# A DMA from SBUF to SBUF in place of PE transposes for the stacked q of a gated linear attention with an MLP

## The chip, the cores and the metric

The kernel runs on one core of a Trainium2 chip. The metric is the device time of one execution in microseconds; the time of a kernel is the median of several executions. A profile is one more execution, with its own time; its page counts from the first to the last instruction, and this stretch is called the span.

## The reference

Batch B = 4, heads H = 8, sequence S = 768, head size D = 48; the MLP works on DM = H * D = 384 and 4 * DM = 1536 columns.

```python
mag = np.sqrt(a_re * a_re + a_im * a_im)
scale = np.minimum(mag, 0.999) / (mag + 1e-06)
a_re_n, a_im_n = (a_re * scale, a_im * scale)
for t in range(S):
    ar, ai = (a_re_n[:, :, t, :, None], a_im_n[:, :, t, :, None])
    new_re = ar * S_re - ai * S_im
    new_im = ar * S_im + ai * S_re
    kv = np.einsum('bhd,bhe->bhde', k[:, :, t], v[:, :, t])
    S_re, S_im = (new_re + kv, new_im)
    y[:, :, t] = np.einsum('bhd,bhde->bhe', q[:, :, t], S_re)
x = y.transpose(0, 2, 1, 3).reshape(B, S, H * D)
mu = np.mean(x, axis=-1, keepdims=True)
var = np.mean((x - mu) ** 2, axis=-1, keepdims=True)
xn = (x - mu) / np.sqrt(var + 1e-06) * g_ln
out = x + np.maximum(xn @ w_ch1, 0.0) @ w_ch2
```

The recurrence has a complex decay per channel; only the real part of the state is read. The inputs and the output are float32.

## The kernel before

The sequence of each batch is cut into chunks of 128 rows (6 a batch, 24 in all, numbered 0 to 23). Three chunks are a unit (UC = 3; 8 units, two a batch, numbered 0 to 7). The recurrence is worked as attention within a chunk and a state from chunk to chunk.

For a unit, `elementwise` computes on ACT and DVE the decay's cumulated magnitude (`ep`, `en`, lines 179 to 185) and phase (`n`, `f`, lines 197 to 208), its cosine and sine, and then writes two stacked tiles in bfloat16: `qstk`, which holds for each of the 128 rows, 3 chunks and 8 heads the 48 values of q times cosine and, after a gap of 16, the 48 of q times sine (128 columns a head, with zeros in the gaps), and `kstk`, the same for k. Lines 233 to 238 write qstk first, then kstk. There are two of each, for even and odd units.

For each chunk:
- `heads_t` (line 245) brings both to a layout with the 128 stacked columns on the partitions. For q, PE transposes the 8 heads into PSUM (`q_ps`, line 250), and ACT copies them to `qt` in SBUF (line 252). For k, PE does 8 more (`k_ps`, line 255), and DVE copies them to `kt` (line 257). `qt` and `kt` have two buffers each.
- `scores` (line 260) multiplies kt with qt for each head (`a_ps`, line 267), and DVE masks the result into `at` (line 269).
- `values` (line 272) adds at times v and qt times the state `s` (`y_ps`, lines 278 and 281), which ACT copies to `x` (line 284), and then makes the next state (`t_ps`, lines 297 to 304). Line 281 is the last that reads a chunk's qt.
- `norm_t` (line 310) takes the mean and variance of x (`stats`, `mv`, `mean`, lines 317 to 320) and transposes x into `xt` (lines 322 to 327).

The MLP runs a unit or two behind: `up` (line 338; `h_ps`, line 344, and its Relu on ACT into `ht`, line 346) for the unit before, and `down` (line 348; `o_ps`, line 352, `o`, line 355, and the DMA to the output, line 358) for the one before that.

The main loop (lines 407 to 435) walks over the chunks in slots; `heads_t` of the next chunk comes between `scores` and `values` of this one, and `advance` and `need` feed in pieces of `elementwise` of later units. A scheduler orders the instructions of each engine when the program is built and adds the waits; on the chip each engine works its list in that order.

SP's DMA queue carries the loads of `a_re` and `a_im` (tiles `ar` and `ai`, lines 100 and 103; each batch's next but one is loaded while the kernel runs), the small copies `edge` (line 189) and the outputs (line 358). POOL's queue loads q, k, v (to bfloat16) and the weights.

Of the kernel before, what the change touches and what calls it, by code (L numbers as in the profile page):

```python
# [10 lines left out]
BF16 = mybir.dt.bfloat16  # L11
# [3 lines left out]
PI = 3.14159265358979323846  # L15
LNCAP = -0.0020010006671670786
MAGIC = 12582912.0
TWO_PI_SAFE = 6.2831845
INV2PI = 1.0 / (2.0 * PI)
NOSYNC = mybir.DependencyInfo(mybir.DependencyClass.NoSync, mybir.DependencyReason.DATA)  # L20
# [3 lines left out]
def kernel(  # L24
# [12 lines left out]
    nc = tc.nc  # L37
    B, H, S, D = q.shape
    C = 128
# [6 lines left out]
    UC = 3  # L46
# [5 lines left out]
    psum = pool("psum", 1, space=bass.MemoryType.PSUM)  # L52
# [9 lines left out]
    ident = consts.tile([C, C], BF16)  # L62
# [48 lines left out]
    for i in range(2):  # L111
        qs = consts.tile([C, UC, H, 2, DP], BF16, name=f"qstk{i}")
        ks = consts.tile([C, UC, H, 2, DP], BF16, name=f"kstk{i}")
# [19 lines left out]
    def table(inst):  # L133
        tc.add_manual_dep(inst.ins, group[0].ins.name, NOSYNC, reason="table order")
        group[1].append(inst.ins)
        return inst
# [15 lines left out]
    def elementwise(b, us, carry):  # L152
# [44 lines left out]
        for st in us:  # L197
            n, f, af = (utile(x, tag="tmp", bufs=4) for x in ("n", "f", "af"))
            for c in range(UC):
# [3 lines left out]
                if carry[0] is not None:  # L203
                    nc.tensor.matmul(ps, lhsT=all_turn, rhs=carry[0], start=False, stop=True)
                nc.vector.tensor_scalar(out=row(n, c), in0=ps, scalar1=MAGIC, scalar2=MAGIC,  # L205
                                        op0=ALU.add, op1=ALU.subtract)
                st["fdone"] = nc.vector.tensor_tensor(out=row(f, c), in0=ps, in1=row(n, c),  # L207
                                                      op=ALU.subtract)
                if st["u"] * UC + c < NCH - 1:
                    if carry[0] is None:  # L210
                        carry[0] = row(st["th"], c)
                    else:
# [7 lines left out]
            sin, cos = utile("sin"), utile("cos")  # L220
            table(nc.scalar.activation(out=sin, in_=f, func=AF.Sin, scale=TWO_PI_SAFE))  # L221
            table(nc.scalar.activation(out=cos, in_=af, func=AF.Sin, scale=-TWO_PI_SAFE,
                                       bias=half_pi))
# [21 lines left out]
    def heads_t(g):  # L245
        st, c = units[g // UC], g % UC
        qs, ks = st["qs"], st["ks"]
        q_ps = psum.tile([C, H, C], BF16, tag="tr", name="q_ps", bufs=2)
        for h in range(H):
            nc.tensor.transpose(q_ps[:, h], qs[:, c, h].rearrange("p a d -> p (a d)"), ident)  # L250
        qt = att.tile([C, H, C], BF16, tag="qt", name="qt")
        nc.scalar.copy(out=qt, in_=q_ps)  # L252
        k_ps = psum.tile([C, H, C], BF16, tag="tr", name="k_ps", bufs=2)
        for h in range(H):
            nc.tensor.transpose(k_ps[:, h], ks[:, c, h].rearrange("p a d -> p (a d)"), ident)  # L255
        kt = att.tile([C, H, C], BF16, tag="kt", name="kt")
        nc.vector.tensor_copy(out=kt, in_=k_ps)  # L257
        chunks[g] = dict(qt=qt, kt=kt)

    def scores(g):  # L260
# [143 lines left out]
    load_weights()  # L404
    load(1, ("q", "k", "v"))
    heads_t(0)
    for s in range(NG + 2 * UC):
        U, c = s // UC, s % UC
        up_u, dn_u = U - 1, U - 2
        hasup, hasdn = 0 <= up_u < NUT, 0 <= dn_u < NUT  # L410
        js = [c * (NJ // UC) + i for i in range(NJ // UC)]
        if s < NG:
            scores(s)
        advance(RATE)
        if hasup:
            up(up_u, js[0])
            up(up_u, js[1])
        if s + 1 < NG:
            need((s + 1) // UC)
            heads_t(s + 1)  # L420
        if s < NG:
            values(s)
            done[0] = (s + 1) // UC
            if s % NCH == NCH - 1:
                load(s // NCH + 2, ("v",))
        advance(RATE)
        if hasup:
            up(up_u, js[2])
            up(up_u, js[3])
        if hasdn:  # L430
            down(dn_u, c)
        if s < NG:
            norm_t(s)
            if s % NCH == HOLD:
                hold_a(s // NCH + 2, mark[0])
# [30 lines left out]
```

## Time and profile before

| | |
|---|---|
| time before, median of 3 | 266.68 us (265.99 to 268.78) |
| profiled execution, its own time | 267.18 us |
| its span | 265.4 us |
| PE busy | 195.5 us (74%) |
| weight loads (PEld) | 128.0 us (48%) |
| DVE busy | 193.1 us (73%) |
| ACT busy | 161.0 us (61%) |
| POOL busy | 49.5 us (19%) |
| transposes of q on PE (L250) | 19.1 us, 192 matmuls |
| evictions of q on ACT (L252) | 24.3 us, 24 copies of 1011 ns |
| DMA, POOL's queue | 76112 packets, 9.44 MB, 62.3% of 16 engines |
| DMA, SP's queue | 25536 packets, 14.18 MB, 23.7% of 16 engines |

A line of the group table gives the source line (L250), the engine, the operation with the tile written and the tiles read, the shapes, the count, then the busy time in us and the mean duration of one in ns, and last the idle time of the engine just before, with what ended most of it. PEld is the load of the stationary operand, which can run beside a matmul. In a line of the timeline the first number is the start in us, the second the duration. In a line of stages, the columns after the length of the stage are each engine's busy us, with the number of instructions, then the TensorE clock that was granted (1.00 is full speed), the busy share of the DMA engines and the GB/s moved. The chain of waits goes back from the last instruction through whatever released each step.

### The profile page before, as it was taken

What the parts mean: (1) busy time and instruction counts of PE and PEld (TensorE: products, weight loads), DVE (VectorE), ACT (ScalarE), POOL (GpSimd) and SP (SyncE); (2) the same over time, 40 slices, a digit from 0 to 9 for tenths busy, and PEclk for the clock granted to TensorE, in tenths of its full rate; (3) what the DMA queues carried; (4) which work ended last, traced back from release to release, by engine and by line L of the source; (5) the groups of instructions that cost most, each with busy time, mean ns of one, the idle gap of its engine ahead of it and who ended that gap; (6) DMA issues with size and microseconds to landing.
All of it is one profiled execution on the core that took longest, in us unless ns stands there. A gap on an engine that the chain in (4) does not pass through costs nothing.

```text
span 265.4 us, 4671 instructions
## 1 busy us (share of the span) xinstructions
PE 195.5 (74%) x1860; PEld 128.0 (48%) x1860; DVE 193.1 (73%) x395; ACT 161.0 (61%) x250; POOL 49.5 (19%) x61
## 2 busy tenths in 40 slices
PE   0012467429782395999998788999977999998994
PEld 0000355217460273666664455666644676764452
DVE  2145896787975989987899979958998876652111
ACT  3244945469995449886973599869636454543320
POOL 9844900035304006001003200010002001001000
PEclk9999999658997579799999689999997999999999
DMA  8999999999989908920379900000100000000012
GB/s 129 149 135 135 181 227 231 204 122 119 131 121 210 140 1 43 159 39 32 91 178 193 77 0 33 30 34 2 61 5 25 32 32 30 33 30 32 30 59 90
DMA packets 102070, 23.91 MB, mean 90 GB/s; under 512 B 87840, under 2 KB 101664, under 8 KB 102048
## 3 DMA queue, kind: packets, MB, share of 16 engines
q0 software_dynamic: 76112, 9.44, 62.3%
q1 hardware_dynamic: 25536, 14.18, 23.7%
q8 instruction: 14, 0.23, 0.3%
q10 hardware_dynamic: 400, 0.00, 0.1%
q14 instruction: 8, 0.07, 0.1%
HBM read 28.31 MB, written 4.72 MB: 124 GB/s over the span
## 4 chain that ended last, share of the span: by engine, by line
PE 38%; ACT 28%; DVE 23%; issue 5%; DMA 3%; SPq 1%; POOLq 0%; POOL 0%; DVEq 0%; ACTq 0%
PE o_ps L352 12%; PE h_ps L344 9%; ACT L128 4%; ACT ht L346 4%; DVE n L205 4%; ACT qt L252 3%; DVE f L207 3%; DMA ai<-in_a_im_dram 3%; ACT ep L184 3%; PE a_ps L267 3%; PE q_ps L250 3%; ACT ai L168 2%; ACT th L195 2%; ACT en L185 2%; PE k_ps L255 2%
## 5 line engine op out<-in xcount | busy, mean ns | idle before, releaser
L344 PE MATMUL h_ps<-xt,w1b 128*128 128x384 bf16 x288 | 63.0, 338 | 5.4 <-ACT ht L346 3.0
L346 ACT ACTIVATE ht<-h_ps 128x384 bf16<-128x384 f32 x96 | 45.8, 496 | 31.6 <-PE h_ps L344 30.7
L352 PE MATMUL o_ps<-w2b,ht 128*128 128x384 bf16 x288 | 51.3, 326 | 1.4 <-ACT ht L346 1.2
L352 PEld LDWEIGHTS <-ht 128*128 128x128 bf16 x288 | 27.8, 97 | 19.4 <-issue 1.9
L344 PEld LDWEIGHTS <-w1b 128*128 128x128 bf16 x288 | 26.1, 100 | 21.9 <-issue 9.6
L355 DVE SCALAR_TENSOR_TENSOR o<-o_ps,rs,x 128x384 f32<-128x384 f32 x24 | 14.8, 615 | 25.4 <-PE o_ps L352 18.1
L269 DVE TENSOR_TENSOR at<-a_ps,mask 128x512 bf16<-128x512 f32 x48 | 31.6, 675 | 1.0 <-PE a_ps L267 1.0
L252 ACT COPY qt<-q_ps 128x1024 bf16<-128x1024 bf16 x24 | 24.3, 1011 | 13.0 <-PE q_ps L250 12.9
L250 PE MATMUL q_ps<-ident,qstk 128*128 128x128 bf16 x192 | 19.1, 251 | 12.5 <-DVE qstk L236 11.6
L257 DVE COPY kt<-k_ps 128x1024 bf16<-128x1024 bf16 x24 | 16.5, 688 | 10.6 <-PE k_ps L255 10.5
L332 POOL TENSOR_SCALAR rs<-mv 128x3 f32<-128x3 f32 x8 | 1.9, 233 | 113.1 <-DVE o L355 80.5
L250 PEld LDWEIGHTS <-qstk 128*128 128x128 bf16 x192 | 15.1, 114 | 16.2 <-DVE qstk L236 14.2
L201 PE MATMUL th_ps<-th,u_turn 128*128 128x384 bf16 x24 | 9.3, 395 | 17.0 <-DVE f L207 8.6
L183 PE MATMUL l_ps<-lm,u_half 128*128 128x384 bf16 x24 | 8.3, 361 | 18.3 <-DVE lm L176 17.4
L278 PE MATMUL y_ps<-v,at 128*128 128x48 bf16 x192 | 16.0, 189 | 6.1 <-DVE at L269 4.9
L221 ACT ACTIVATE sin<-f 128x1152 bf16<-128x1152 bf16 x8 | 9.3, 1163 | 15.7 <-DVE f L207 11.9
L284 ACT CAST x<-y_ps 128x384 bf16<-128x384 f32 x24 | 11.6, 484 | 11.3 <-PE y_ps L278 11.2
L278 PEld LDWEIGHTS <-at 128*128 128x128 bf16 x192 | 12.6, 99 | 11.7 <-DVE at L269 9.3
L255 PE MATMUL k_ps<-ident,kstk 128*128 128x128 bf16 x192 | 17.6, 245 | 0.8 <-DVE kstk L236 0.6
L267 PE MATMUL a_ps<-qt,kt 128*128 128x128 bf16 x192 | 17.2, 234 | 0.7 <-DVE kt L257 0.4
L184 ACT ACTIVATE ep<-l_ps 128x384 bf16<-128x384 f32 x24 | 12.2, 508 | 9.1 <-PE l_ps L183 9.0
L165 DVE TENSOR_TENSOR r<-ai,rec 128x1152 bf16<-128x1152 f32 x8 | 10.8, 1350 | 9.3 <-DMA ai<-in_a_im_dram 9.3
(77 smaller groups left out, 383.4 us busy)
## 6 DMA issues: line engine op xcount, KB each, us to landing
out_dram<-o SPq DMA_DIRECT2D x24, 192.0 KB, 1.9
q<-in_q_dram POOLq DMA_DIRECT2D x3, 576.0 KB, 10.5
k<-in_k_dram POOLq DMA_DIRECT2D x3, 576.0 KB, 11.1
v<-in_v_dram POOLq DMA_DIRECT2D x3, 576.0 KB, 9.1
ar<-in_a_re_dram SPq DMA_DIRECT2D x6, 192.0 KB, 3.5
ai<-in_a_im_dram SPq DMA_DIRECT2D x6, 192.0 KB, 8.3
w1b<-in_moe_w_ch_dram POOLq DMA_DIRECT2D x1, 1152.0 KB, 13.6
w2b<-in_moe_w_ch_dram POOLq DMA_DIRECT2D x1, 1152.0 KB, 22.0
```

The costliest lines, as they stand in the source:

```text
L184: table(nc.scalar.activation(out=row(ep, c), in_=ps, func=AF.Exp))
L250: nc.tensor.transpose(q_ps[:, h], qs[:, c, h].rearrange("p a d -> p (a d)"), ident)
L252: nc.scalar.copy(out=qt, in_=q_ps)
L255: nc.tensor.transpose(k_ps[:, h], ks[:, c, h].rearrange("p a d -> p (a d)"), ident)
L257: nc.vector.tensor_copy(out=kt, in_=k_ps)
L267: nc.tensor.matmul(a_ps[:, j], lhsT=ch["kt"][:, h], rhs=ch["qt"][:, h], start=True, stop=True)
L269: nc.vector.tensor_tensor(out=at[:, ts(i, H // 2)], in0=a_ps, in1=mask_b, op=ALU.mult)
L278: nc.tensor.matmul(y_ps[:, h], lhsT=ch["at"][:, h], rhs=vt[:, h, gb], start=True, stop=sp is None)
L344: nc.tensor.matmul(h_ps, lhsT=w1b[:, i, ts(j, C)], rhs=st["xt"][:, i], start=(i == 0), stop=(i == ND - 1))
L346: nc.scalar.activation(out=st["ht"][:, j], in_=h_ps, func=AF.Relu)
L352: nc.tensor.matmul(o_ps, lhsT=st["ht"][:, j, ts(c, C)], rhs=w2b[:, j], start=(j == 0), stop=(j == NJ - 1))
L355: nc.vector.scalar_tensor_tensor(out=o, in0=o_ps, scalar=st["rs"][:, ds(c, 1)], in1=chunks[U * UC + c]["x"], op0=ALU.mult, op1=ALU.add)
```

## The change

From unit 1 on (chunks 3 to 23), the stacked q of a chunk, 128 rows by 8 heads of 128 columns, is transposed by one DMA on SP's queue from `qstk` straight into `qt`. The 8 PE transposes, their PSUM tile and the copy by ACT are gone for these chunks. The first three chunks, and k in all chunks, stay as they were. In the changed file the DMA has line 253.

```diff
+XBAR = (0,)
...
     def heads_t(g):
         st, c = units[g // UC], g % UC
         qs, ks = st["qs"], st["ks"]
-        q_ps = psum.tile([C, H, C], BF16, tag="tr", name="q_ps", bufs=2)
-        for h in range(H):
-            nc.tensor.transpose(q_ps[:, h], qs[:, c, h].rearrange("p a d -> p (a d)"), ident)
         qt = att.tile([C, H, C], BF16, tag="qt", name="qt")
-        nc.scalar.copy(out=qt, in_=q_ps)
-        k_ps = psum.tile([C, H, C], BF16, tag="tr", name="k_ps", bufs=2)
-        for h in range(H):
-            nc.tensor.transpose(k_ps[:, h], ks[:, c, h].rearrange("p a d -> p (a d)"), ident)
         kt = att.tile([C, H, C], BF16, tag="kt", name="kt")
-        nc.vector.tensor_copy(out=kt, in_=k_ps)
+        for i, (o, x) in enumerate(((qt, qs), (kt, ks))):
+            if g >= UC and i in XBAR:
+                nc.sync.dma_start_transpose(out=o, in_=x[:, c].rearrange("p h a d -> p (h a d)"))
+                continue
+            t_ps = psum.tile([C, H, C], BF16, tag="tr", name="qk_ps", bufs=2)
+            for h in range(H):
+                nc.tensor.transpose(t_ps[:, h], x[:, c, h].rearrange("p a d -> p (a d)"), ident)
+            if i == 0:
+                nc.scalar.copy(out=o, in_=t_ps)
+            else:
+                nc.vector.tensor_copy(out=o, in_=t_ps)
         chunks[g] = dict(qt=qt, kt=kt)
```

## The prediction

> **What bounds the kernel now.** I read the page first (busy shares, slices, groups), then the chain of waits by stage, then the busy time of stages, and last the timeline around the start of a unit, because there the stacked q is finished just before it is used.
>
> ```profile
> PE 195.5 (74%) x1860; PEld 128.0 (48%) x1860; DVE 193.1 (73%) x395; ACT 161.0 (61%) x250; POOL 49.5 (19%) x61
> ...
> L252 ACT COPY qt<-q_ps 128x1024 bf16<-128x1024 bf16 x24 | 24.3, 1011 | 13.0 <-PE q_ps L250 12.9
> L250 PE MATMUL q_ps<-ident,qstk 128*128 128x128 bf16 x192 | 19.1, 251 | 12.5 <-DVE qstk L236 11.6
> ```
>
> No engine bounds the whole span: PE and DVE are both near 73%. The removed work is in the two last lines: 19.1 us of PE and 24.3 us of ACT for 24 chunks. The busy time of four stages (the columns are us of the stage, then PE, PEld, DVE, ACT, POOL) tells where that work counts:
>
> ```profile
> 61.00:91.00 30.00, 18.50 (x187) 11.32 (x187) 24.53 (x49) 23.89 (x39) 8.03 (x6) 0.84 1.82 153
> 94.00:141.00 47.00, 43.17 (x438) 29.13 (x437) 42.41 (x85) 37.99 (x61) 6.29 (x5) 0.94 0.72 84
> 150.00:180.00 30.00, 27.76 (x284) 18.46 (x282) 25.29 (x49) 25.60 (x43) 1.11 (x2) 0.93 0.06 21
> 210.00:236.00 26.00, 25.91 (x307) 18.22 (x306) 16.62 (x38) 12.88 (x24) 1.11 (x2) 1.00 0.09 32
> ```
>
> From 210 on PE alone is full. From 94 to 180 PE and DVE are both near 90%. From 61 to 91 DVE and ACT are at 80% and wait for each other. Next, the timeline at the start of unit 4 (start, us, engine, line):
>
> ```profile
> 140.70 0.75 DVE L236 TENSOR_TENSOR qstk<-qe,sin 128x1152 bf16<-128x1152 bf16 x1
> ...
> 142.04 0.75 DVE L236 TENSOR_TENSOR kstk<-ke,sin 128x1152 bf16<-128x1152 bf16 x1
> ...
> 143.91 0.68 DVE L257 COPY kt<-k_ps 128x1024 bf16<-128x1024 bf16 x1
> ...
> 144.64 0.45 PEld L267 LDWEIGHTS <-kt 128*128 128x128 bf16 x8 [0.50 <-DVE kt L257]
> ```
>
> qstk is complete at 141.45, but the scores (L267) start only at 144.64, when kt is there. So a new way for q has a cover of 3.1 us: the k path takes that long anyway. Units 1, 2 and 6 look the same (qstk 58.40, 90.84, 193.91; kt done 61.56, 94.00, 197.04). Units 3, 5 and 7 have their qstk 12 us or more early (unit 3 at 102.5 against L250 at 117.2).
>
> **The change, part by part.** *Removed:* for 21 of 24 chunks 8 transposes (19.1/24 = 0.80 us of PE) and one eviction (1.01 us of ACT), in all 16.7 us of PE and 21.2 us of ACT. What of it sets the end, by stage:
> - 210 to 236: the L250 rows in this stage are 2.60 us of PE, and PE is full: 2.6 us.
> - 150 to 180: the chain of this stage gives 13.1% to qt and 3.7% to q_ps, 5.0 us together. The k transposes and kt follow a step later and take part of it over; the PE time removed is 2.55. Between the two: 3.8 us.
> - 94 to 141: 3.2% and 2.8% of 47 us, 2.8 us. DVE is 90% busy and is not relieved: half, 1.4 us.
> - 61 to 91: one qt of 0.90 us lies on the chain: half, 0.5 us.
>
> The sum is 8.3 us, at most 11.3 if nothing takes the place of the removed pieces.
>
> *Added:* 21 transposing DMAs of 256 KB on SP's queue. The trace has no such transfer, so its time T from issue to landing has to be bounded:
>
> ```profile
> out_dram<-o SPq DMA_DIRECT2D x24, 192.0 KB, 1.9
> ...
> ar<-in_a_re_dram SPq DMA_DIRECT2D x6, 192.0 KB, 3.5
> ...
> k<-in_k_dram POOLq DMA_DIRECT2D x6, 96.0 KB, 10.2
> ```
>
> The fastest neighbour is the output row: 1.9 us for 192 KB in 1536-byte packets, scaled by bytes 2.5 us. The slowest is the POOL row: 10.2 us for 1024 packets, behind others. The nearest is ar (L103): the same queue and 1024 runs, as a transpose of 128 rows times 8 heads has; 3.5 us, or 4.7 scaled by bytes. I take 4.1 us and keep 2.5 and 10 for the range. About 1.4 us of it is fixed (the output's 1.9 less 9 packets an engine of 60 ns), 2.7 us is data.
>
> The Trainium skill bears on this term ("VectorE: DVE Perf Modes", "The three transpose paths"): it lists 1309 ns for a 128x128 transpose by the DMA crossbar against 390 ns on TensorE, which speaks against the change. Eight in a row would be 10.5 us, an estimate from that page; the sum would then be the second rival's. No transposing DMA is in this trace.
>
> *Stalls.* Where T exceeds the cover, L267 waits, and behind it in PE's order stand th_ps, y_ps and h_ps; DVE's at (L269) waits with it.
> - Unit 6: DMA idle: 4.1 - 3.1 = 1.0 us.
> - Unit 2: the load of v on POOL's queue still runs until about 93; two us of shared engines cost about 1.0: 1.9 us.
> - Unit 1: the same with v and q: 2.0 us.
> - Unit 4: the load of ai (L100) is issued on SP at 136.0, lands 8.3 us later (the median of ai), and stands ahead on the same queue; less 0.9 us to land, its packets end at 143.4. Then 2.7 us of own data, 1.0 for sharing with v, 1.0 to land: 148.1 against 144.6, 3.5 us.
>
> The sum is 8.4 us. In units 4 and 6 DVE works off n, o, f and stats between a_ps and at, so 1.2 and 1.0 us of the wait cost nothing: 6.2 us are left.
>
> *Other chunks:* a transpose can start when the buffer is free, that is when y_ps (L281) two chunks earlier is done. From there to the scores is 7.4 us at the least (chunk 10: 119.2 to 126.6; chunk 15: 7.5; most 8 to 11). With T = 4.1 these are hidden; the second chunk of a unit (10 us after the first at unit 2) is too.
>
> *SP's queue:* in the built order the 21 transposes stand between the 24 output DMAs, the edge copies and the loads of ar and ai. The output of chunk 11 (o at 198.1) now stands behind a transpose that waits for y_ps of chunk 18 (201.6): 3.5 us late; its buffer is wanted again at 216. The loads of ar and ai for batch 2 stand behind the transpose of chunk 5, free at 67.5, and were issued at 75.3. No cost.
>
> *PE's order* changes too: the scores of chunk 4 stand behind 15 h_ps matmuls that they stood ahead of. The same work; counted as nothing, 2 us either way.
>
> The sum: 265.4 - 8.3 + 6.2 = 263.3 us of span. The profiled execution took 267.18, 1.8 more than its span, and was 0.5 above the median of 266.68: 263.3 + 1.8 - 0.5 = **264.6 us**, 0.8% faster. About 1% (2.7 us) is what a measurement of this kernel can tell from no change.
>
> **The rivals.** *The DMA is hidden everywhere, and all of the gain comes.* T is near 2.5, only unit 4 waits about 1 us, and the whole 11.3 us of the chain go: 265.4 - 11.3 + 1.0 + 1.3 = 256.4. For it: in 150 to 180 the chain is full of qt, and DMA is idle. Against: kt must wait for PE and DVE as before.
>
> *A slow transfer becomes the bound at the start of units (slower).* One mechanism: a longer T makes the four waits grow faster than the gain (each us of T costs nearly 4; it decides from T = 5.3 on, where 2.1 us of gain have become 2.7 of loss). At T = 10 units 1, 2, 4, 6 wait 6.9, 6.8, 7.2 and 5.7, 26.6 us; the second chunks of units 1 and 2 queue behind the first (3.6 + 2.5), and chunks with leads of 7.4 to 9.8 us come late by 7.9 in all: 40.6 - 8.3, or 299 us. T = 7 gives about 276. For it: 1024 packets on POOL's queue took 10.2 us, and each partition of the result gets its elements from 128 partitions, which no transfer in this trace does. Against: those 10 us were behind others.
>
> *PE's waits bring the clock down (slower).* These two stages, one after an idle PE (4.41 us before L250 in unit 1), one without:
>
> ```profile
> 58.00:62.00 4.00, 3.06 (x24) 2.40 (x25) 2.59 (x5) 3.99 (x5) 3.83 (x4) 0.50 2.36 79
> ...
> 141.00:146.00 5.00, 3.67 (x35) 2.11 (x34) 5.00 (x10) 1.07 (x2) 1.66 (x1) 1.00 1.65 183
> ```
>
> At clock 0.50 eight transposes take 1.03 us in place of 0.62. If unit 4 waits 3.5 us and falls to 0.50 for the next 4 us of PE work, and units 1 and 2 stay low 2 us longer, that is 4 + 2 + 2 = 8 us: 272.6. By the skill ("TensorE: Matmul & The Clock Gate", Part 1) one idle window of about 3.4 us halves the clock; the trace agrees at unit 1, but before unit 2 an idle of 2.35 us is already followed by 0.50. By that rule unit 4 alone would pay.
>
> **How the numbers follow.** Forecast 0.42, its own range 259 to 271 (T 3.5 to 5.3, gain 6 to 11): 0.17 of it faster by over 1%, 0.18 within, 0.07 slower. Hidden 0.18, all faster. Slow transfer 0.28, clock 0.12, both slower. So faster 0.35, same 0.18, slower 0.47. The cases of both signs are near each other in weight, so the range goes from the hidden case, 256, into the slow one, 290 (T about 9).
>
> **What would show it.** Right: the transposes land in 3.5 to 5 us with DMA otherwise idle; L267 of units 1, 2, 4 waits for the DMA by 1 to 4 us, and for no other chunk by over 1; from 210 to 236 a slot takes 5.9 us in place of 6.5; DVE busy stays near 193, ACT falls to 140, PE to 179. Wrong: landing above 5.3 us, L267 waiting for a DMA at most chunks, a granted clock of 0.50 behind unit 4, or a late load of ar or ai.

## The result and the profile after

The changed kernel took 274.56 us (median of 4, 273.25 to 275.58), the kernel before 266.34 us in the same comparison; the ratio is 1.029, with a 95% interval of 1.021 to 1.038. A later comparison (*after_again*) gave 271.97 us against 267.11 us, 1.019 (1.015 to 1.022). Some executions took over 1.5% longer than the fastest of their kernel; medians and ratios here leave them out. The change makes the kernel slower by 2 to 3%, where 0.8% faster was forecast. The profiled execution took 273.92 us, with a span of 272.1 us.

The page of the changed kernel, engines and two groups:

```profile
PE 188.6 (69%) x1692; PEld 120.4 (44%) x1692; DVE 194.0 (71%) x395; ACT 143.0 (53%) x229; POOL 49.5 (18%) x61
...
L257 PE MATMUL qk_ps<-ident,kstk 128*128 128x128 bf16 x192 | 19.2, 256 | 9.8 <-DVE kstk L237 9.8
...
L271 PE MATMUL a_ps<-qt,kt 128*128 128x128 bf16 x192 | 17.9, 238 | 7.8 <-DMA qt<-qstk 7.6
```

The work is gone as meant: 168 matmuls fewer, and ACT is busy for 18 us less. What is new stands at the end of the last line: PE was idle for 7.6 us before the scores, waiting for the transposing DMA. The answer on DMA for the same kernel (KB each, then median us from issue to landing; the row of qt has no KB):

```profile
out_dram<-o SPq DMA_DIRECT2D x24, 192.0 KB, 1.9
...
v<-in_v_dram POOLq DMA_DIRECT2D x3, 576.0 KB, 12.7
ar<-in_a_re_dram SPq DMA_DIRECT2D x6, 192.0 KB, 3.7
...
k<-in_k_dram POOLq DMA_DIRECT2D x6, 96.0 KB, 10.2
...
qt<-qstk SPq DMA_TRANSPOSE x21, 2.8
```

The nine landings that the trace tells have a median of 2.8 us, near the lower bound of 2.5. But the longest of them took 8.1 us (chunk 5, whose scores did not wait), and the first chunk of unit 4, where the scores do wait, shows what such a landing costs. Its timeline (start, us, engine, line; what an instruction waited for is in brackets):

```profile
147.56 2.30 POOL L101 DMA_DIRECT2D v<-in_v_dram  x1 [17.12 <-PE h_ps L348]
...
149.03 0.76 DVE L237 TENSOR_TENSOR qstk<-qe,cos 128x1152 bf16<-128x1152 bf16 x1
...
149.84 3.84 SPq L253 DMA_TRANSPOSE qt<-qstk  x2
150.36 0.76 DVE L237 TENSOR_TENSOR kstk<-ke,sin 128x1152 bf16<-128x1152 bf16 x1
...
152.23 0.69 DVE L261 COPY kt<-qk_ps 128x1024 bf16<-128x1024 bf16 x1
...
154.36 0.55 DVE L321 BATCH_NORM_STATS2 stats<-x 128x6 f32<-128x384 bf16 x1
...
157.17 1.01 PE L271 MATMUL a_ps<-qt,kt 128*128 128x128 bf16 x8 [4.31 <-DMA qt<-qstk]
157.79 0.69 DVE L273 TENSOR_TENSOR at<-a_ps,mask 128x512 bf16<-128x512 f32 x1 [2.88 <-PE a_ps L271]
...
157.97 0.53 PE L202 MATMUL th_ps<-th,u_turn 128*128 128x384 bf16 x1
```

kt is there at 152.9, the scores start at 157.17. The transpose was issued at 149.84, and 2.3 us before it the load of v for batch 3 had gone to POOL's queue. Behind the scores in PE's list stands a `th_ps` (157.97), which needs no qt; DVE, which lives on it, ran out of work at 154.9. In the trace's DMA packets the load's begin first: the transpose's first packet starts at 152.46, its last ends at 155.61. The chain of waits of that stretch puts the transpose at 7.19 us:

```profile
149.84 7.19 DMA qt<-qstk
157.03 0.14 issue
157.17 1.01 PE a_ps L271 x8
```

Three stages of this kernel (us of the stage, then PE, PEld, DVE, ACT, POOL, granted clock, DMA share, GB/s). What was 210 to 236 lies 7 us later here:

```profile
217.00:243.00 26.00, 25.87 (x292) 17.97 (x291) 17.77 (x41) 9.66 (x20) 1.11 (x2) 1.00 0.25 62
```

And the wait of unit 4 with what follows it:

```profile
150.00:157.00 7.00, 2.28 (x19) 1.19 (x16) 4.91 (x10) 0.00 (x0) 0.00 (x0) 0.89 1.69 121
157.00:163.00 6.00, 4.49 (x40) 3.44 (x41) 4.83 (x11) 2.48 (x3) 1.39 (x2) 0.50 0.91 125
```

PE is still full at the end; behind unit 4's wait the granted clock is 0.50. PE's busy time fell by 6.9 us in all (195.5 to 188.6), not by the 16.7 that were removed; the mean granted clock of the profiled execution is 0.880, where the kernel before had 0.923.

The best map of gains and losses is when each chunk's scores start, against the kernel before (us, from the timelines of one execution each; the kernels of the other columns follow below):

| scores of chunk | before, at | after | e1 | e15 | e11c | e3 | e7 | e14 |
|---|---|---|---|---|---|---|---|---|
| 3 (unit 1) | 61.6 | +2.0 | +0.7 | +1.5 | +2.5 | +1.6 | -0.3 | -0.6 |
| 6 (unit 2) | 94.3 | +4.2 | +2.0 | +4.3 | +3.0 | +2.0 | -0.6 | +0.1 |
| 9 (unit 3) | 120.7 | +7.5 | +3.1 | +4.5 | +3.6 | +2.3 | -0.1 | +1.5 |
| 12 (unit 4) | 144.6 | +12.5 | +3.9 | +6.1 | +4.4 | +3.1 | -0.4 | +3.1 |
| 15 (unit 5) | 171.4 | +12.1 | +4.3 | +3.9 | +4.5 | +3.2 | -0.2 | +1.6 |
| 18 (unit 6) | 197.1 | +9.6 | +1.8 | +1.3 | +6.1 | +0.6 | -2.8 | -0.9 |
| 23 (last) | 235.7 | +7.0 | +0.2 | -0.3 | +3.8 | -1.0 | -4.4 | -3.4 |

One execution is not the next: in the profile of *after_again* (271.54 us) chunk 9 starts 4.6 us later than before, not 7.5. Most of the difference lies between the chunks 6 and 9 (29.7 us here, 26.8 there), where the clock is at 0.50 from 111.1 to 118.0 here and only from 109.2 to 112.6 there. Unit 4's wait is in both (4.31 and 4.59 us).

### The profile page after: what moved, and what is told of

Read it like the earlier page. It is cut to its first block, busy times and chain, and to the rows that moved or that the text cites. A ratio compares the mean times of both kernels' runs of the same rounds, so it can differ in the third digit from the quotient of the medians.

```text
span 272.1 us, 4342 instructions
## 1 busy us (share of the span) xinstructions
PE 188.6 (69%) x1692; PEld 120.4 (44%) x1692; DVE 194.0 (71%) x395; ACT 143.0 (53%) x229; POOL 49.5 (18%) x61
## 5 line engine op out<-in xcount | busy, mean ns | idle before, releaser
L348 PE MATMUL h_ps<-xt,w1b 128*128 128x384 bf16 x288 | 64.9, 348 | 7.2 <-ACT ht L350 4.8
L348 PEld LDWEIGHTS <-w1b 128*128 128x128 bf16 x288 | 26.7, 101 | 24.9 <-issue 13.5
L359 DVE SCALAR_TENSOR_TENSOR o<-o_ps,rs,x 128x384 f32<-128x384 f32 x24 | 14.8, 617 | 26.0 <-PE o_ps L356 16.7
L257 PE MATMUL qk_ps<-ident,kstk 128*128 128x128 bf16 x192 | 19.2, 256 | 9.8 <-DVE kstk L237 9.8
L288 ACT CAST x<-y_ps 128x384 bf16<-128x384 f32 x24 | 11.4, 477 | 22.9 <-PE y_ps L282 18.8
L271 PE MATMUL a_ps<-qt,kt 128*128 128x128 bf16 x192 | 17.9, 238 | 7.8 <-DMA qt<-qstk 7.6
L202 PE MATMUL th_ps<-th,u_turn 128*128 128x384 bf16 x24 | 9.8, 416 | 18.2 <-ACT th L196 10.2
L257 PEld LDWEIGHTS <-kstk 128*128 128x128 bf16 x192 | 15.6, 118 | 13.1 <-DVE kstk L237 11.8
L282 PE MATMUL y_ps<-v,at 128*128 128x48 bf16 x192 | 16.9, 192 | 5.6 <-DVE at L273 4.3
L282 PEld LDWEIGHTS <-at 128*128 128x128 bf16 x192 | 13.6, 102 | 13.5 <-DVE at L273 8.7
L271 PEld LDWEIGHTS <-kt 128*128 128x128 bf16 x192 | 14.0, 107 | 12.0 <-issue 8.2
L261 DVE COPY kt<-qk_ps 128x1024 bf16<-128x1024 bf16 x24 | 16.5, 686 | 3.2 <-PE qk_ps L257 2.9
L206 DVE TENSOR_SCALAR n<-th_ps 128x384 bf16<-128x384 f32 x24 | 13.2, 555 | 6.1 <-PE th_ps L205 5.4
L166 DVE TENSOR_TENSOR r<-ai,rec 128x1152 bf16<-128x1152 f32 x8 | 10.8, 1352 | 9.3 <-DMA ai<-in_a_im_dram 9.2
## 6 DMA issues: line engine op xcount, KB each, us to landing
q<-in_q_dram POOLq DMA_DIRECT2D x3, 576.0 KB, 15.3
v<-in_v_dram POOLq DMA_DIRECT2D x3, 576.0 KB, 12.7
```

What stands on the lines that cost most here:

```text
L166: nc.vector.tensor_tensor(out=st["r"], in0=ai, in1=st["rec"], op=ALU.mult)
L257: nc.tensor.transpose(t_ps[:, h], x[:, c, h].rearrange("p a d -> p (a d)"), ident)
L261: nc.vector.tensor_copy(out=o, in_=t_ps)
L271: nc.tensor.matmul(a_ps[:, j], lhsT=ch["kt"][:, h], rhs=ch["qt"][:, h], start=True, stop=True)
L282: nc.tensor.matmul(y_ps[:, h], lhsT=ch["at"][:, h], rhs=vt[:, h, gb], start=True, stop=sp is None)
L348: nc.tensor.matmul(h_ps, lhsT=w1b[:, i, ts(j, C)], rhs=st["xt"][:, i], start=(i == 0), stop=(i == ND - 1))
```

## The experiments

Times are medians in us; the ratio is to the kernel before in the same comparison.

| run | what it is | time | before | ratio (95%) |
|---|---|---|---|---|
| e1_v_later | v's loads held back | 267.0 | 267.4 | 0.998 (0.994, 1.001) |
| e4_traffic_only | before + unread transposes | 267.1 | 267.4 | 0.999 (0.997, 1.001) |
| e11c_spare_load_before | e1 + unread load at unit 6 | 270.12 | 267.11 | 1.012 (1.008, 1.017) |
| e5_first_on_pe_v_later | e1 + e2 | 266.27 | 267.26 | 0.995 (0.992, 0.998) |
| e3_q_free | q not transposed | 264.78 | 267.4 | 0.991 (0.987, 0.994) |
| e7_q_free_order_back | e3, order back | 264.02 | 267.26 | 0.987 (0.984, 0.990) |
| e2_first_on_pe | DMA for chunks 2 and 3 of a unit | 265.12 | 267.4 | 0.993 (0.989, 0.996) |
| e6_v_later_order_back | e1, order back | 265.25 | 267.26 | 0.991 (0.987, 0.995) |
| e10_first_on_pe_order_back | e2, order back | 264.70 | 268.08 | 0.990 (0.986, 0.993) |
| e12_before_order_back | before, the same edit | 267.42 | 268.08 | 0.998 (0.996, 1.000) |
| e15_order_back_only | after, order back | 266.83 | 267.11 | 0.999 (0.996, 1.002) |
| after_again | after | 271.97 | 267.11 | 1.019 (1.015, 1.022) |
| e8_clock_held | after + 56 transposes of identity | 271.30 | 268.08 | 1.013 (1.008, 1.018) |
| e13_order_only | the same with 1 | 268.28 | 267.78 | 1.000 (0.997, 1.004) |
| e9_q_and_k_not_first | e2 with k too | 266.33 | 267.26 | 0.995 (0.992, 0.999) |
| e14_from_unit_2 | e6, unit 1 on PE | 263.27 | 267.78 | 0.983 (0.980, 0.987) |

### Is it the transfer beside a load?

Theory A: a transpose is fast alone and slow beside a load on POOL's queue, and the first chunk of a unit has no lead. *e1_v_later* moves the loads of v for batches 2 and 3 by a slot, with a memset of one column on DVE in front of them (in the profiles they are issued at 112.2 and 165.3 in place of 81.5 and 147.6):

```diff
-            if s % NCH == NCH - 1:
-                load(s // NCH + 2, ("v",))
...
+            if s and s % NCH == 0:
+                hold_v(s // NCH + 1, mark[0])
```

> The changed kernel, with the loads of v for batches 2 and 3 held back by a slot, so that they no longer run at the starts of units 2 and 4. Theory A (loads on POOL's queue and the transposes slow each other; the waits at the starts of units and the lower clock behind them are the loss): the transposes of chunks 6 and 12 land in 2.7 to 3.5 us in place of 4.9 and 7.2, the scores there wait under 0.5 us in place of 1.8 and 4.3, the granted clock behind unit 4 is 1.00, and the time is 266 to 269 us. Theory B (the loss is the new order of instructions on PE, DVE and ACT): the waits may go, but the time stays at 272 to 275.

267.0 us: the loss is gone, within the interval. Of three waits only unit 1's is left. Unit 4's transpose, issued at 145.44, no longer holds the scores; its PE timeline:

```profile
147.97 0.32 PE L202 MATMUL th_ps<-th,u_turn 128*128 128x384 bf16 x1 [0.58 <-DVE f L208]
148.13 0.32 PE L205 MATMUL th_ps<-carry,all_turn 128*128 128x384 bf16 x1
148.57 0.62 PE L271 MATMUL a_ps<-qt,kt 128*128 128x128 bf16 x8
```

*e4_traffic_only* asks whether the traffic itself costs anything: the kernel before, plus the 21 transposes into a tile that nothing reads.

```diff
+        if g >= UC:
+            nc.sync.dma_start_transpose(out=spare, in_=qs[:, c].rearrange("p h a d -> p (h a d)"))
```

> The kernel before, with the 21 transposing DMAs added, into a spare tile that nothing reads; PE and ACT still do the work for q. Theory A: nothing waits for the transposes, the loads on POOL's queue are late by up to 5 us but have more slack than that: 265 to 268 us. Rival (the traffic itself slows loads that the kernel waits for, whoever waits for the transposes): 270 us or more.

267.1 us, no change. SP's queue and the DMA engines carry the 21 transposes for nothing; only what waits for them can cost.

e1 takes a load away; the counter-test adds one where there was none. *e11_v_later_spare_load* and *e11b_spare_load_in_time* are e1 with an unread load of v near unit 6:

```diff
+            if s == 17:
+                spare = ins.tile([C, H, NCH, D], BF16, tag="v", name="v")
+                m = nc.vector.memset(spare[:, 0, 0, 0:1], 0.0)
+                tc.add_manual_dep(m.ins, mark[0].ins.name, NOSYNC, reason="load order")
+                nc.gpsimd.dma_start(out=spare, in_=src(v, B - 1))
```

> e1_v_later, and besides, a load of v that nothing reads is issued on POOL's queue just ahead of the transpose of unit 6's first chunk (its tile is the one of v of batch 2, free by then). In e1 that transpose has DMA to itself and lands in 2.9 us. Theory A (a transpose beside a casting load takes 5 to 8 us, and the first chunk has no lead): it lands 6 to 8 us after its issue, the scores of chunk 18 wait for it by 3 to 4.5 us as those of unit 4 did in the changed kernel, of which about 1 is made up by DVE: 269.5 to 271. Rival (unit 4's wait had another cause, such as ai's load ahead on the queue or the clock): at most 1 us more, 267 to 268.

> As e11_v_later_spare_load, but the load that nothing reads goes to the tile of q of batch 2, which is free long before, so that it is issued 2 us ahead of the transpose of unit 6's first chunk (in the last try it was issued at 204.5, when that transpose had landed: 267.4, no loss, and nothing told). Theory A: the transpose lands 6 to 8 us after its issue, the scores of chunk 18 wait for it by 3 to 4.5 us, 269 to 271.5. Rival (unit 4's wait had another cause): at most 1 us of wait, 267 to 268.

266.94 and 266.77 us, but neither told anything: the loads were issued at 204.54 and 206.22, long after the transpose (194.98 and 196.91). *e11c_spare_load_before* has `if s == 16:` and the buffer of q's tag, which puts the load ahead.

> As e11_v_later_spare_load, with the load that nothing reads placed behind xt of chunk 16 on DVE, ahead of unit 5's rs on POOL: issued at about 192.6, 3 us ahead of the transpose of unit 6's first chunk (the two tries before issued it at 204.5 and 206.2, behind a tile that came free late and behind rs, and told nothing). Theory A: the transpose lands 5 to 8 us after its issue in place of 2.9, the scores of chunk 18 wait by 2.5 to 4.5 us, the time is 2 to 4 us above e1_v_later's 267.0: 269 to 271. Rival (unit 4's wait had another cause): no wait over 1 us, 267 to 268.

270.12 us, 3.1 above e1. Unit 6, which waited for a DMA in no other run, now does what unit 4 did. The load in POOL's timeline:

```profile
193.09 2.31 POOL L451 DMA_DIRECT2D spare<-in_v_dram  x1 [15.11 <-DVE spare L449]
```

The scores of chunk 18 in PE's timeline:

```profile
203.22 1.01 PE L271 MATMUL a_ps<-qt,kt 128*128 128x128 bf16 x8 [4.27 <-DMA qt<-qstk]
```

The chain of waits there:

```profile
195.94 7.14 DMA qt<-qstk
203.08 0.14 issue
203.22 1.01 PE a_ps L271 x8
```

7.14 us from issue to landing in place of some 2.9, a wait of 4.27 us, and 3.1 to 3.6 us of time (the table's last row, +3.8 against +0.2). Theory A is shown for the wait: it is the load, not the place. What the wait costs depends on the order behind it, as the section on the order shows.

### What is the removed work worth?

*e3_q_free* leaves out the transposition of q from unit 1 on: the scores and the state's part read a tile of constants. It estimates what a transposition at no cost can bring.

```diff
+    qconst = consts.tile([C, H, C], BF16, name="qconst")
+    nc.gpsimd.memset(qconst, 0.01)
...
-        qt = att.tile([C, H, C], BF16, tag="qt", name="qt")
+        qt = att.tile([C, H, C], BF16, tag="qt", name="qt") if g < UC else qconst
...
-                nc.sync.dma_start_transpose(out=o, in_=x[:, c].rearrange("p h a d -> p (h a d)"))
```

> The whole gain by itself: from unit 1 on q is not transposed at all, the scores and values read a tile of constants in its place, and neither PE, ACT nor DMA does anything for q. Theory A: the gain is what the chain gave to q_ps and qt, 8.3 us (at most 11.3): 255 to 258 us. Theory B, or a k path that takes the place of all of it: 263 us or more.

264.78 us: 2.6 us, a third of the 8.3. 1.6 us are lost at the start, where the memset of the constants stands in POOL's way. Of the rest, the table's column e3 shows a loss of 1.1 us from chunk 6 to 12, where 1.4 of gain were forecast. DVE's timeline there:

```profile
134.96 0.56 DVE L322 BATCH_NORM_STATS2 stats<-x 128x6 f32<-128x384 bf16 x1 [0.69 <-ACT x L289]
135.54 0.56 DVE L309 TENSOR_TENSOR s<-t_ps,dec 128x384 bf16<-128x384 f32 x1
136.01 0.55 DVE L206 TENSOR_SCALAR n<-th_ps 128x384 bf16<-128x384 f32 x1
```

and the kernel before:

```profile
132.64 0.56 DVE L205 TENSOR_SCALAR n<-th_ps 128x384 bf16<-128x384 f32 x1 [0.18 <-PE th_ps L204]
133.15 0.56 DVE L317 BATCH_NORM_STATS2 stats<-x 128x6 f32<-128x384 bf16 x1
```

Without the removed instructions the scheduler puts `n` of unit 4 behind `stats` and `s`, and so behind ACT's x; DVE idles and unit 4 is stacked later. This is theory O. The changed kernel, e1 and e2 have the same order there. The edit for it writes two pieces of unit 4 ahead of the values of chunk 10:

```diff
+        if s == 10:
+            advance(2)
         if s < NG:
             values(s)
```

*e7_q_free_order_back* is e3 with it and the constants filled on DVE.

> e3_q_free (from unit 1 on q is not transposed at all; the scores and the state's part read a tile of constants), with that tile filled on DVE in place of POOL, which put the start back by 1.6 us, and with the order of e6_v_later_order_back. This is the most that a transposition at no cost can bring. Theory O: 264.8 - 1.6 - 1.8, 261 to 262. Rival (the order is nothing, only the late start was an artefact): 263 to 263.5. Against both, the prediction's gain of 8.3 us would give 257 to 258.

264.02 us, 3.2 below before: theory O's 261 to 262 is missed, and the rival's figures by half a microsecond. In its profile the stretch from chunk 9 to 18 wins 2.7 us where e3 won 1.6, and the start is not late, but its median is only 0.8 below e3's. The profiled execution was its quickest (262.77), so I go by the median. The transposition of q is worth about 3 us to this kernel, not 8. This is no strict bound, since the scheduler orders each kernel anew: e14 below, which does transpose q, has a ratio of 0.983, and the intervals overlap.

*e2_first_on_pe* keeps the first chunk of each unit on PE and ACT:

```diff
-            if g >= UC and i in XBAR:
+            if g >= UC and c > 0 and i in XBAR:
```

> The changed kernel, but the first chunk of every unit keeps the PE transposes and the copy by ACT; the DMA serves the second and third chunks alone (14 of 24), which have 7 us and more until their scores. Theory A: no scores wait for a DMA; two thirds of the gain of 8.3 us stay, 5.5, so 260 to 263 us, faster than before the change. Theory B: 268 us or more.

265.12 us, with no wait for a DMA: a gain, but below the 5.5 us that were expected; with q free, too, only 2.6 came. *e5_first_on_pe_v_later* adds e1's edit.

> The first chunk of each unit keeps the transposes on PE and ACT, its other two chunks have the transposing DMA (14 in all), and the loads of v for the batches 2 and 3 are held one slot back as in e1_v_later. Theory A (the loss is the wait behind a v load at the first chunk of a unit, and nothing else that hangs on the loads): e2_first_on_pe has no wait of the scores for a DMA left, so the later loads add nothing, 264.5 to 266. Rival (the loads also slow transposes that are not the first of their unit, or other transfers of that time): 262 to 263.5, with the transposes landing faster than in e2_first_on_pe.

266.27 us, no better than e2: the later loads bring nothing by themselves, so what e1 wins over the changed kernel (5.0 to 7.6 us by its two medians) comes with the waits that they remove.

### The order around the wait

*e6_v_later_order_back*, *e10_first_on_pe_order_back* and the control *e12_before_order_back* put `advance(2)` into e1, e2 and the kernel before.

> e1_v_later, and besides, two pieces of the elementwise work of unit 4 are written ahead of the values of chunk 10, so that on DVE n stands ahead of that chunk's stats and s again, as in the kernel before. Theory O (1.8 us of the gain are lost between chunks 9 and 12 because the scheduler, without the instructions that fell away, puts n behind work that waits for ACT's x): the stretch from chunk 9 to chunk 12 gives back 1 to 2 us, 265 to 266. Rival (that stretch is long for another reason, PE's own or the loads): no change, 267 +- 0.5.

> e2_first_on_pe (the first chunk of each unit on PE and ACT, the other two by DMA) with two pieces of unit 4's elementwise work written ahead of the values of chunk 10, as in e6_v_later_order_back. Theory O: what e6 and e7_q_free_order_back won between the chunks 9 and 18 by that order (2.0 and 1.9 us) comes here too: 263 to 264, and a start of chunk 18 at 190.8 to 191.3 where e2 has 192.8. Rival (the order matters only where the first chunks come by DMA): 265 +- 0.5.

> The kernel before with the same edit of order as e10_first_on_pe_order_back and nothing else: the control of theory O. Theory O (the changed kernel lost an order that the kernel before has): no gain here, 267 to 268, or a loss of some us where the pieces come too early. Rival (the edit is a gain of its own that has nothing to do with the transposes): 265 to 265.5.

265.25 (1.75 below e1, as expected), 264.70 (a ratio of 0.990 where e2 has 0.993, so 0.8 us, less than expected, with overlapping intervals) and 267.42 (within 1 us of before: the edit is hardly a gain of its own). Theory O holds in sign, and in size for e6, but not in its place: in the profiles e6 takes 25.5 us from chunk 9 to 12 where e1 takes 24.7, and wins from 12 to 18 (47.7 against 50.3). There the clock is a rival: in e6, e10 and e12 it stays at 1.00 behind chunk 12, while e1 has 0.50 from 150.2 to 157.0, e2 from 150.0 to 153.4 and the kernel before from 147.4 to 154.3. So the gain of `advance(2)` can be clock as well as order; no run separates them.

Next, the wait itself. *e8_clock_held* fills unit 4's wait with 56 transposes of the identity, to ask for the clock; *e13_order_only* has one in place of 56. In both the first scores of chunk 12 come behind x_ps of chunk 11 and both th_ps pieces:

```diff
+        if g == 12:
+            d_ps = psum.tile([C, H, C], BF16, tag="tr", name="d_ps", bufs=2)
+            for i in range(56):
+                last = nc.tensor.transpose(d_ps[:, i % H], ident, ident)
```

> The changed kernel with 56 transposes of the identity, which nothing reads, on PE between unit 4's k transposes and its scores, so that PE isn't idle while it waits for the DMA. Theory C (the wait also brings the granted clock to 0.50 behind unit 4, and that is a large part of the loss): the same wait, the clock 1.00 from 157 to 163, 2 to 3 us less than the changed kernel's 274.6. Theory A (the wait itself is the loss; before and e1 fall to 0.50 there too): within 1 us of 274.6.

> e8_clock_held with one transpose of the identity in place of 56: PE has the same order up to the scores of chunk 12 (both th_ps pieces and x_ps of chunk 11 ahead of them, where the changed kernel has the second th_ps piece and x_ps behind them), but is idle through the wait. Theory Q (e8's 3.3 us came from the order: DVE's elementwise work goes on during the wait, since what it needs is no longer queued behind the waiting scores): 271 to 272. Theory C (they came from the clock held at 1.00): 274 to 275, with a clock of 0.50 from 157 to 163.

271.30 and 268.28 us: the order alone gives back the whole loss within the interval (ratio 1.000), more than theory Q's 271 to 272, and with the clock held the time is 3.0 us longer. The slow transfer is still there: e8's lines of POOL and SP show the load 2.3 us ahead of the transpose, as in the changed kernel.

```profile
143.77 2.30 POOL L101 DMA_DIRECT2D v<-in_v_dram  x1 [17.12 <-PE h_ps L358]
```
```profile
146.05 3.62 SPq L254 DMA_TRANSPOSE qt<-qstk  x2
```

The transpose's last packet ends 5.6 us after its issue in e8, 5.8 us in the changed kernel. So, by e13, most of what the wait costs comes from what stands behind the waiting scores; its executions spread widely, from 265.8 to 269.6 us. e8's clock was 1.00 from 157 to 163, but its helpers kept PE until 157.6, so it doesn't price the clock; holding it in this way brings nothing beyond the order.

*e15_order_back_only* is the changed kernel with `advance(2)` and nothing else, *after_again* the changed kernel beside it.

> The changed kernel with two pieces of unit 4's elementwise work written ahead of the values of chunk 10 (the edit of e6_v_later_order_back alone; the loads of v stay where they are). On PE both th_ps pieces of that time then stand ahead of the scores of chunk 12. Theory Q (a large part of the loss is what is queued behind the waiting scores, and 1.8 us more is the order between the chunks 9 and 12): 4 to 6 us less than after_again, 269 to 271. Rival (only the wait itself counts): 1.5 to 2 us less, 272.5 to 273.

> The changed kernel as it is, on the same chip as the two others and with more runs than it had: 273.5 to 275.5 by every theory.

266.83 against 271.97 us: 5.1 us, within theory Q's 4 to 6, though both came lower than written (2.2 and 1.5 us below their bands). Yet this run does not show theory Q by itself. Its edit names no load, but it changes who comes first: the transpose is now issued 0.65 us ahead of v's load, and its last packet ends at 149.18, as the load's first starts. The two no longer meet. SP's and POOL's lines:

```profile
145.53 3.65 SPq L253 DMA_TRANSPOSE qt<-qstk  x2
```
```profile
146.18 2.30 POOL L101 DMA_DIRECT2D v<-in_v_dram  x1 [18.71 <-PE h_ps L348]
```

Unit 4 in e15's timeline, DVE first:

```profile
142.75 0.75 DVE L237 TENSOR_TENSOR qstk<-qe,cos 128x1152 bf16<-128x1152 bf16 x1
143.42 0.61 DVE L359 SCALAR_TENSOR_TENSOR o<-o_ps,rs,x 128x384 f32<-128x384 f32 x1
...
144.00 1.28 DVE L273 TENSOR_TENSOR at<-a_ps,mask 128x512 bf16<-128x512 f32 x2
...
146.33 0.75 DVE L237 TENSOR_TENSOR kstk<-ke,sin 128x1152 bf16<-128x1152 bf16 x1
```
PE's lines of the same unit:

```profile
150.46 0.32 PE L202 MATMUL th_ps<-th,u_turn 128*128 128x384 bf16 x1 [1.64 <-DVE f L208]
150.62 0.32 PE L205 MATMUL th_ps<-carry,all_turn 128*128 128x384 bf16 x1
150.79 0.61 PE L271 MATMUL a_ps<-qt,kt 128*128 128x128 bf16 x8
```
And the stage (columns as above, the granted clock third from the end):

```profile
150.00:154.00 4.00, 2.30 (x31) 1.72 (x31) 3.88 (x10) 1.28 (x2) 1.12 (x2) 1.00 1.74 133
```

qstk is complete at 143.5, the scores start at 150.8: the cover has grown from 3.1 to 7.3 us, because o, at and xt now lie between q's stacking and k's, and both th_ps pieces stand ahead of the scores. These scores wait for no DMA, and the clock stays at 1.00. So the 5.1 us hold three things at once: no meeting with the load, a longer cover and no fall of the clock.

### Versions

*e9_q_and_k_not_first* transposes k by DMA too, in the second and third chunks (`XBAR = (0, 1)` on e2).

> The second and third chunk of each unit from unit 1 on have both q and k transposed by DMA (28 in all), the first chunk keeps PE, ACT and DVE for both. It takes 14 x 0.69 us of copies off DVE and as many transposes off PE. Theory D (with q gone the chunk's chain stands on the way of k over PE and DVE, so what a chunk wins is bounded by it): 261 to 264, faster than e2_first_on_pe by 1 to 4 us, most of it in the last stage, where the loads are over. Rival (two transposes one after the other on one queue need 5.5 us and over 8 beside the loads, more than the lead that a second chunk has): a wait for kt at the second chunks, 267 to 272.

266.33 us: between the two, and no better than e2, though DVE is busy for 9 us less (184.4 against 193.6). Its second chunk of unit 4 meets the load:

```profile
153.53 0.61 PE L271 MATMUL a_ps<-qt,kt 128*128 128x128 bf16 x4 [4.61 <-DMA kt<-kstk]
```

*e14_from_unit_2* is e6 with unit 1 left on PE and ACT (`g >= 2 * UC`).

> e6_v_later_order_back with the DMA from unit 2 on, unit 1 on PE and ACT as in the kernel before: it takes away the last wait for a transposing DMA that e6 has (unit 1, 3.1 us in its profile). If that wait is worth what it lasts less 1 us: 263 to 264. If in this stretch DVE and ACT set the time anyway: 265 to 265.5.

263.27 us, as expected for a wait that is worth what it lasts less 1 us, and 1.7% (1.3 to 2.0) faster than before: the fastest of all, and faster than both kernels. No scores wait for a DMA.

## Why the prediction was wrong, step by step

- **T alone: too high.** 4.1 us taken, 2.7 to 2.8 measured, near the output's row scaled by bytes rather than ar's. The parts differ too: 1.1 us of packets, not 2.7, and 0.5 us from the last packet to landing, not 0.9 to 1.0 (chunk 10: issued at 126.03, packets from 127.22 to 128.30, landed at 128.76). The scores of unit 6 did not wait; 1.0 us was forecast for them, at no price.
- **Sharing with a load: mis-sized.** 1.0 us taken; 7.2 measured less 2.7 alone is 4.5 us (unit 4, and e11c's 7.1). That the wait at unit 4 came out near, 4.31 against 3.5, is luck, because two errors met: the term for ai ahead on the queue was not there (ai was issued at 142.0, the transpose at 149.84).
- **The waits came out well in sum:** 1.42, 1.82 and 4.31 us at units 1, 2 and 4 are 7.6 us, where 2.0, 1.9, 3.5 and 1.0 were given, and no other chunk waited. Their price was put at 6.2; against the kernels without q (264.0 and 264.8) the changed kernel's two medians are 7.2 to 10.5 us longer, with the new order and the clock in it.
- **The gain: the term that failed most.** 8.3 us forecast, 2.6 to 3.2 measured with q free. 210 to 236 came nearest (2.6 us forecast; from chunk 18 to 23 2.6 us in the changed kernel, 1.6 in e3, e7 and e1), though a slot took 6.2 in place of 6.6 and not 5.9. The other stages were read as if the pieces of the chain that are removed were time saved. They aren't, as e7's profile shows: from chunk 12 to 18 it wins 2.4 us where 3.8 was forecast for 150 to 180, and from 6 to 12 nothing where 1.4 was. In its chain from 149.6 to 177 qt and q_ps are gone, but DVE's r (L166) has 9.2% and idle issue 11.4%, where the kernel before has 4.2 (L165) and 3.0% in 150 to 180.
- **"The same work; counted as nothing, 2 us either way":** this failed too. The scheduler's new order leaves x_ps and th_ps behind the waiting scores of unit 4. e13 brings them ahead, with the load where it was, and is 3.7 to 6.3 us below the changed kernel's two medians. Where no load delays the transpose, e6 against e1, the order (or the clock with it) is worth 1.75 us, with intervals that touch. The prediction named th_ps behind L267 and drew no price from it.
- **SP's queue at no cost:** right as far as the runs go (e4; and in the changed kernel no wait for ar or ai is longer than before).
- **The rivals.** The slow transfer (slower) named the right place and the right neighbours, but T is long only beside loads (4.4 to 8.1 us in the changed kernel), and 2.7 to 3.3 elsewhere, as far as the trace tells landings. The clock rival's 272.6 us is near the measured time, but not for its reason alone: the clock did fall to 0.50 behind unit 4, as in the kernel before between 150 and 154, and stayed low longer (10.2 against 6.8 us), yet e8 with the clock at 1.00 there took 271.3. The prediction also read the trace wrongly here: the clock was at 0.50 from 48.5 and from 82.6 on, ahead of the idle times of 4.41 and 2.35 us (from 54.05 and 88.55) that it named, so neither shows what brings it down. How much of e15's 5.1 us is the clock, how much the order and how much the load stays open. It stays open too why the restored order gave e7 and e10 less than e6.

The Trainium skill ("VectorE: DVE Perf Modes", "The three transpose paths") led to an estimate of 10.5 us for eight heads at 1309 ns; the trace differs, with 2.7 us for all eight heads in one DMA, and decides. The Trainium skill ("DMA: Bandwidth & Descriptors", "Queues, rings and completion order") says that each DMA engine takes turns between the queues that have work, packet by packet. The trace agrees in kind: from 153 to 155 unit 4's transpose moved 848 packets of 256 B and v's load 929 of 96 B, while a transpose alone (e1, 151.5 to 152.0) moved 567 in half a microsecond.

## What to carry to other kernels

A DMA that takes over work from an engine needs a lead at its tightest point, and its time has to be taken beside the loads that run just then, not alone: here 2.7 us became 7.2. Ask what else stands behind the waiting instruction in its engine's list: moving independent work ahead of it (e13), holding the load back (e1), or an order in which the transpose is through before the load starts (e15) each undid the loss, within the intervals. And price removed work by a kernel that leaves it out: 38 us of PE and ACT were worth 3.

## What the hardware showed unexpectedly

- A transpose of 128 x 1024 bfloat16 (256 KB) from SBUF to SBUF takes 2.7 us from issue to landing when DMA is otherwise idle: 1.2 us to the first packet, 1.1 us of packets, 0.5 us to landing (chunk 10). SP is held for 1.26 us (median) by each issue.
- It moves as packets of 256 B: the page's count on this queue grew by 22176 for 21 transposes, 1056 each. In the trace a packet took 18 ns alone and 31 ns beside v's load, whose packets of 96 B took 28 to 30 ns.
- The load suffers as well: the median landing of v's loads went from 9.1 to 12.7 us, and that of q's from 10.5 to 15.3. In e4 they were 11.4 and 12.5, and the time was that of the kernel before.
- In the 20 profiles the granted clock changes on a grid of 3.41 us. From 30 us after the start to 5 us before the end, each of the 105 falls to 0.50 follows a step of the grid in which PE was busy for 53% or less, and each of the 105 rises one of 81% or more. So a fall needs no idle stretch: in the kernel before PE was busy for 1.80 us of 144.03 to 147.44, with no idle time over 0.9 us, and the clock fell at 147.44. Some steps of 37 to 53% brought no fall.
